# A written order of all five engines, from the first gate tile through the second chunk of a linear-attention and gated-feed-forward kernel

## The chip, the cores and the metric

One core of a Trainium2 chip runs the whole kernel. The metric is the device time of one execution in microseconds; the time of a kernel is the median of several. The core has five engines that each work through their own list of instructions in order: PE (TensorE, matmul; its weight loads are counted apart as PEld), DVE (VectorE), ACT (ScalarE), POOL (GpSimd) and SP (SyncE, which here issues all DMAs). They wait for each other on semaphores.

## The reference

```python
def _attn_ref(q, k, v):                 # (batch 8, heads 8, seq 576, head_dim 64)
    q_s = exp(q - max(q, axis=-1));  q_s = q_s / (sum(q_s, axis=-1) + 1e-09)
    k_s = exp(k - max(k, axis=2));   k_s = k_s / (sum(k_s, axis=2) + 1e-09)
    kv = einsum('bhsd,bhse->bhde', k_s, v)
    return einsum('bhsd,bhde->bhse', q_s, kv)

x = attn_out.transpose(0, 2, 1, 3).reshape(4608, 512)
a = x @ w_a                             # 512 x 1536
b = x @ w_b                             # 512 x 1536
out = (a * b) @ w_out                   # 1536 x 512
```

Everything is float32; the weights arrive as 64-bit floats, and the kernel turns them into float32 itself.

## The kernel before

**Tiling.** The 4608 rows of x are cut into nine chunks of 512. The 1536 inner columns are cut into twelve tiles f of 128 (six pairs i). For precision a float32 operand is split into two parts in a format that PE reads fast ("hi" and "lo", `split`: a copy on ACT, a subtraction on DVE), and a product is three matmuls: hi·hi, hi·lo, lo·hi.

**Start-up and first chunk (chunk 0).** `Startup` is a class of small steps, named by two letters and numbers (`wl20`: the lo part of weight tile 2, first half). They are traced in the order of a hand-written string: keys (`mc`, `ek`, `tr`, `pk`, `kv`), queries (`qs`, `qe`, `pq`, `px`), operands of x (`xh`, `xl`), weights (`wc`, `ws`, `wa`, `wo`, `wh`, `wl`: the conversion of one 128 x 512 block goes ACT, DVE, POOL, DVE, ACT, DVE) and the first three gate tiles (`g`, `ga`, `G`).

Then a loop over f = 2 to 11 does for each f:

- load the raw weights of tile f + 2 (`load_f`; three loads of 512 KB on SP);
- convert weights: `convert_wo(f)` for the output weights, `convert_ab(f + 1, 0)` and `(f + 1, 1)` for the two gate halves;
- of a task n = f - 3 the transposes ("turn"), of task n + 1 the softmax ("soft"); the nine tasks are key pairs 0 to 3 and query pairs 0 to 3 of the second chunk, and one key pair of the third;
- the gate tile f: 24 matmuls of 128 x 512 into two banks (`gate_part`, twelve for a, twelve for b), ACT copies a out (`gate_half`), DVE multiplies by b (`gate_end`);
- the product of task n ("prod"), and the projection of tile f - 1 into four banks (`project_first`, four float32 matmuls).

**From the second chunk on (chunks 1 to 8)** a pair i takes seven half-size products (`product`, twelve matmuls of 128 x 256 each) into banks kx, ky, ka and kp, with sums and products on DVE (u2, u3, cc), a hi/lo split (`g_split`) and a projection of twelve matmuls a tile (`project`). Between them `attend` (a `Spread`) traces a share of the attention of the chunk after. In chunk 1 the operands S1 to S4 are sums of weight blocks that POOL adds (`sums`) and that ACT and DVE split.

**What sets the order.** A scheduler orders the traced instructions by a timeline of its own and by priorities. Three things bound it: `in_order` chains what lies in a stretch of the trace by dependences without a semaphore, so that an engine takes it in the order of the code (ACT, DVE and POOL in the hand-written start-up, SP in its loads, PE from the start to the end of the first chunk); `tc.issue_after(x)` lets what is traced in it go only behind x (weights of tile f + 1 behind the end of gate tile f - 2, the softmax likewise, and in `attend` the attention pieces behind the last DVE operation of the products); and the buffers.

Of the kernel before, what the change touches and what calls it, by code (L numbers as in the profile page):

```python
# [25 lines left out]
P1, P6, P7, P5, P2, P3, P4 = range(7)  # L26


@with_exitstack
def linear_attention_then_gated_ffn(  # L30
# [570 lines left out]
    xfs = {}  # L601
# [91 lines left out]
    class Spread:  # L693
# [5 lines left out]
        def __call__(self, behind=None):  # L699
# [3 lines left out]
            with ExitStack() as pinned:  # L703
                if behind is not None:
# [284 lines left out]
    traced = nc.cur_bb.bb.instructions  # L989
    by_hand = len(traced)  # L990
    for step in (
# [9 lines left out]
        getattr(Startup, name)(*(int(n) for n in step[len(name):]))  # L1001
# [20 lines left out]

    in_order((E.SP,), loads, by_hand)
    in_order((E.Activation, E.DVE, E.Pool), by_hand, len(traced))
    startup = [at["last", 0].ins, at["last", 1].ins]
# [3 lines left out]
    for f in range(2, NF):  # L1029
        if 1 < f - 1 < NF - 3:  # L1030
            tasks[f - 1][0]()
        if f + 2 < NF:
            load_f(f + 2)

        with tc.issue_after(at["end", f - 2].ins):
            convert_wo(f)
            if f + 1 < NF:
                convert_ab(f + 1, 0)
                convert_ab(f + 1, 1)


        n = f - 3
        if n < 0:
            copies = ()
        else:
            copies = tasks[n][2]()
        if n + 1 < NF - 3:
            with tc.issue_after(startup[0]), tc.issue_after(at["end", max(f - 2, 1)].ins):
                tasks[n + 1][1]()
        if f == NF - 1:  # L1050
            with tc.issue_after(at["end", f - 1].ins):
                split_wo(0)
                split_wo(1)
            sy[0] = sums(0)
        if f > 2:
            pts = gate_banks(("k0", "k1"))
            for h in range(2):
                gate_part(f, x0, h, range(NP), pts[h])
                if h == 0:
                    with ExitStack() as pinned:  # L1060
                        for copy in copies or ():
                            pinned.enter_context(tc.issue_after(copy.ins))
                        at["ga", f] = gate_half(f, pts[0])
            at["end", f] = gate_end(at["ga", f], pts[1])
        if 0 <= n < len(tasks):
            tasks[n][3]()
        if f == NF - 2:
            x_operands(xfs[1], early + late, xo)
        project_first(*pending, po)
        pending = (f, at["ga", f])  # L1070
    in_order((E.PE,), by_hand, len(traced))
# [15 lines left out]
    for c in range(1, NCH):  # L1087
# [4 lines left out]
        for i in range(NI):  # L1092
            def operand(op):
                if c > 1:
                    return get_w(i, op)
                if op in (A11, A12, A22):
                    return get_w(i, op)
                w = split_w(sy[i][op])
                put_w(i, op, w)
                return w  # L1100

            if more and i == NI - 1:
                x_operands(xfs[c + 1], early, xo)
# [5 lines left out]
            u3 = sb.tile([P, 2, H], F32, name="u3", bufs=1)  # L1109
            if c > 1 or i > 0:  # L1110
                attend(last)
# [92 lines left out]
```

## Time and profile before

| | |
|---|---|
| median of 3 runs | 964.56 us (964.27 to 965.41) |
| profiled execution, its own time | 966.23 us |
| its span, first to last instruction | 964.4 us |
| mean granted clock of PE | 0.998 |
| busy in the span: PE / PEld / DVE / ACT / POOL | 932.9 / 828.2 / 624.6 / 391.5 / 105.5 us |
| DMA read and written | 241.40 MB, 37.98 MB |

The profile is one execution, taken by the hardware's profiler. A timeline row gives start and duration in microseconds, engine, line of the kernel, operation, what it writes and reads, its size, how many follow each other, and in brackets the idle time of that engine just before, with what ended it. Line numbers are those of the kernel before: L537 is the gate matmul, L572 the projection of the first chunk, L562 the half-size products, L583 the projection of the later chunks, L846 and L299 key transposes, L314 the key product, L468 and L904 query transposes, L481 the query product, L271 a product with ones that spreads a maximum; L946 and L82 are lo splits on DVE, L548 the gate product, L292 and L385 maxima of a softmax, L110 the addition on POOL in a weight conversion, L225 the sums of weight blocks.

### The profile page before, as it was taken

What the parts mean: (1) busy time and instruction counts of PE and PEld (TensorE: products, weight loads), DVE (VectorE), ACT (ScalarE), POOL (GpSimd) and SP (SyncE); (2) the same over time, 40 slices, a digit from 0 to 9 for tenths busy, and PEclk for the clock granted to TensorE, in tenths of its full rate; (3) what the DMA queues carried; (4) which work ended last, traced back from release to release, by engine and by line L of the source; (5) the groups of instructions that cost most, each with busy time, mean ns of one, the idle gap of its engine ahead of it and who ended that gap; (6) DMA issues with size and microseconds to landing.
All of it is one profiled execution on the core that took longest, in us unless ns stands there. A gap on an engine that the chain in (4) does not pass through costs nothing.

```text
span 964.4 us, 17587 instructions
## 1 busy us (share of the span) xinstructions
PE 932.9 (97%) x6479; PEld 828.2 (86%) x6479; DVE 624.6 (65%) x1209; ACT 391.5 (41%) x1085; POOL 105.5 (11%) x88
## 2 busy tenths in 40 slices
PE   5899999899999999999999999999999999999998
PEld 3656656889999999989999999999999999999997
DVE  7987878886686747665566657566666547553433
ACT  7787744452372416322443244223622263221111
POOL 1544342422000000000000000000000000000000
PEclk9999999999999999999999999999999999999999
DMA  9999686989998968897799779877987689667761
GB/s 348 412 381 390 214 274 214 407 276 332 323 357 297 359 238 273 305 368 256 258 330 356 268 244 351 316 280 258 344 304 286 240 289 305 243 236 266 258 211 56
DMA packets 97588, 282.64 MB, mean 293 GB/s; under 512 B 11680, under 2 KB 12256, under 8 KB 97504
## 3 DMA queue, kind: packets, MB, share of 16 engines
q1 hardware_dynamic: 97504, 281.52, 81.6%
q8 instruction: 52, 0.85, 0.3%
q14 instruction: 32, 0.26, 0.1%
HBM read 241.40 MB, written 37.98 MB: 290 GB/s over the span
## 4 chain that ended last, share of the span: by engine, by line
PE 79%; DVE 7%; DMA 5%; issue 4%; POOL 2%; ACT 2%; SPq 1%; DVEq 0%; POOLq 0%
PE po L583 27%; PE kp L562 13%; PE ka L562 13%; PE kx L562 13%; PE ky L562 7%; POOL wr L110 2%; PE px L493 2%; PE pk L314 2%; DMA ws<-dw 1%; DMA raw<-in_w_ab 1%; DVE wy L113 1%; PE pt L537 1%; DMA ws_y<-dy 1%; SPq L448 1%; DMA kt_first<-in_kt 1%
## 5 line engine op out<-in xcount | busy, mean ns | idle before, releaser
L583 PE MATMUL po<-wo_w,gh 128*128 128x512 f32 x768 | 226.3, 395 | 1.0 <-ACT gh L79 1.0
L562 PE MATMUL kx<-xo,ws 128*128 128x256 f32 x1152 | 162.7, 283 | 0.0
L583 PEld LDWEIGHTS po<-wo_w,gh 128*128 128x128 f32 x768 | 138.6, 188 | 27.6 <-ACT gh L79 1.5
L562 PE MATMUL ka<-xo,ws 128*128 128x256 f32 x1152 | 160.9, 282 | 0.4 <-DVE cc L1147 0.4
L562 PE MATMUL kp<-xo,ws 128*128 128x256 f32 x1152 | 157.6, 283 | 1.5 <-DVE u L1120 1.5
L562 PEld LDWEIGHTS ka<-xo,ws 128*128 128x128 f32 x1152 | 149.5, 188 | 4.7 <-DVE cc L1147 0.6
L562 PEld LDWEIGHTS kp<-xo,ws 128*128 128x128 f32 x1152 | 147.7, 188 | 5.2 <-issue 1.6
L562 PEld LDWEIGHTS kx<-xo,ws 128*128 128x128 f32 x1152 | 149.5, 188 | 2.5
L583 PE MATMUL po<-wo_w,gl 128*128 128x512 f32 x384 | 136.4, 396 | 0.0
L79 ACT CAST gh<-cc 128x512 fp32r<-128x512 f32 x96 | 56.6, 620 | 134.5 <-DVE cc L1144 128.2
L1143 DVE TENSOR_TENSOR cc<-kp,u 128x512 f32<-128x512 f32 x48 | 33.1, 689 | 99.1 <-PE kp L562 98.9
L1134 ACT COPY cc<-kx 128x256 f32<-128x256 f32 x48 | 17.8, 371 | 182.9 <-PE kx L562 182.8
L583 PEld LDWEIGHTS po<-wo_w,gl 128*128 128x128 f32 x384 | 71.2, 188 | 16.0 <-DVE gl L82 0.4
L407 ACT ACTIVATE qt<-qt,st 128x64 f32<-128x64 f32 x224 | 75.0, 339 | 22.4 <-DVE st L404 17.2
L1133 DVE TENSOR_TENSOR cc<-kp,u 128x512 f32<-128x512 f32 x48 | 33.1, 689 | 76.1 <-PE kp L562 75.9
L562 PE MATMUL ky<-xo,ws 128*128 128x256 f32 x576 | 77.6, 284 | 3.2 <-DMA ws<-dw 2.2
L562 PEld LDWEIGHTS ky<-xo,ws 128*128 128x128 f32 x576 | 71.9, 188 | 4.5 <-DVE gl L82 2.1
L82 DVE TENSOR_TENSOR gl<-cc,gh 128x512 fp32r<-128x512 f32 x96 | 64.6, 692 | 10.6 <-ACT gh L79 10.6
L537 PE MATMUL pt<-xo,ws 128*128 128x512 f32 x288 | 70.2, 399 | 1.1 <-DVE ws L946 1.1
L244 POOL PARTITION_ALL_REDUCE mx<-m x20 | 18.3, 915 | 446.5 <-DVE m L255 446.5
L537 PEld LDWEIGHTS pt<-xo,ws 128*128 128x128 f32 x288 | 53.5, 189 | 14.0 <-DVE ws L946 1.6
L1119 ACT COPY u<-kx 128x512 f32<-128x512 f32 x48 | 28.0, 584 | 84.6 <-PE kx L562 84.3
(147 smaller groups left out, 1155.6 us busy)
## 6 DMA issues: line engine op xcount, KB each, us to landing
ws<-dw SPq DMA_DIRECT2D x312, 512.0 KB, 5.5
dw<-ws SPq DMA_DIRECT2D x42, 512.0 KB, 7.2
mr<-dq SPq DMA_DIRECT2D x112, 128.0 KB, 4.6
raw<-in_w_ab SPq DMA_DIRECT2D x24, 512.0 KB, 8.0
out<-ot SPq DMA_DIRECT2D x36, 256.0 KB, 4.7
vt<-in_v SPq DMA_DIRECT2D x28, 325.0 KB, 6.9
qt<-in_q SPq DMA_DIRECT2D x32, 256.0 KB, 5.5
kt<-in_k SPq DMA_DIRECT2D x24, 320.0 KB, 5.1
```

Source lines behind the costliest of these rows:

```text
L79: nc.scalar.copy(out=hi, in_=src)
L82: return nc.vector.tensor_tensor(out=lo, in0=src, in1=hi.bitcast(F32), op=ALU.subtract)
L110: nc.gpsimd.tensor_tensor(out=r, in0=u, in1=r, op=ALU.add)
L314: nc.tensor.matmul(pk[h * D:(h + 1) * D], kt[:, j, h], vt[:, j, h], start=(j == 0), stop=(j == J - 1),)
L407: nc.scalar.activation(out=qt[:, j, h], in_=qt[:, j, h], func=AF.Exp, bias=st[:, h, 0, j:j + 1], accum_out=st[:, h, 1, j:j + 1],)
L493: nc.tensor.matmul(px[:, s], w, m[:, s], start=(i == 0), stop=(i == 2))
L537: nc.tensor.matmul(pt, w[:, wp], x[g][:, xp], start=(g == 0 and i == 0), stop=(g == NP - 1 and i == 2),)
L562: ins = nc.tensor.matmul(pt[:, n], w[:, n, wp, c], x[:, xp, c], start=(first and n == 0 and i == 0), stop=(i == 5), skip_group_check=True,)
L583: ins = nc.tensor.matmul(po[t], a[:, ts], wo[f][:, w], start=(f == 0 and i == 0), stop=(f == NF - 1 and i == 2),)
L1119: nc.scalar.copy(out=u2, in_=kx)
L1133: nc.vector.tensor_tensor(out=cc[:, 3], in0=kp, in1=u3, op=ALU.add)
L1143: nc.vector.tensor_tensor(out=cc[:, 1], in0=kp, in1=u2, op=ALU.add)
```

## The change

Every piece that is traced from the start-up on gets a name (`named`): the step's own name in the start-up; `load.f`, `raw.f`, `out.f`, `a.f`, `b.f`, `turn.n`, `soft.n`, `split.m`, `sums.i`, `gate.f`, `prod.n`, `x.1`, `proj.f` in the loop; and in chunks 1 and 2 `w<op>.i`, `pair.i`, `proj.i`, `attend.i` and so on, with i counted on from 0 to 11. `ORDER` holds for each of the five engines a list of these names; `name*3` takes the next three instructions of that piece on that engine, `name:9` the one that stands tenth among those left. `arrange` chains an engine's instructions in the order of its list; what the list leaves out of the rest of the program goes behind its last entry, in the scheduler's order. The `issue_after` pins of the loop are gone, and `attend` is pinned only from chunk 2 on. No instruction is added, removed or changed on any engine, and no buffer.

```diff
+ORDER = {
+    "PE": (
...
+        "gate.10:9 turn.7*4 gate.10:9 gate.10:9 gate.10:9 proj.8 gate.10*12 proj.8 proj.9:1 proj.9:2 "
...
+    "Activation": (
...
+        "turn.5 b.10 soft.7 soft.7:1 turn.6 soft.7 split.9 soft.7:1 b.11 soft.7:2 out.11 soft.7:2 "
...
+    @contextmanager
+    def named(name):
+        before = traced[-1]
+        yield
+        start = next(n for n in reversed(range(len(traced))) if traced[n] is before) + 1
+        for ins in traced[start:]:
+            work.setdefault((ins.engine, name), []).append(ins)
...
-    in_order((E.SP,), loads, by_hand)
-    in_order((E.Activation, E.DVE, E.Pool), by_hand, len(traced))
...
+    def behind_each_other(instructions):
+        for ins, before in zip(instructions[1:], instructions):
+            tc.add_manual_dep(ins, before.name, ..., reason="in order")
+
+    def arrange(engine, names):
+        left = {name: list(found) for (of, name), found in work.items() if of == engine}
+        chain = []
+        for item in names.split():
+            name, _, count = item.partition("*")
+            name, _, place = name.partition(":")
+            for _ in range(int(count or 1)):
+                chain.append(left[name].pop(int(place or 0)))
+        behind_each_other(chain)
+        placed = {ins.name for ins in chain}
+        for ins in traced[by_hand:]:
+            if ins.engine == engine and ins.name not in placed:
+                behind_each_other([chain[-1], ins])
+
+    behind_each_other([ins for ins in traced[loads:by_hand] if ins.engine == E.SP])
...
-        with tc.issue_after(at["end", f - 2].ins):
+        with named(f"out.{f}"):
             convert_wo(f)
...
-            with tc.issue_after(startup[0]), tc.issue_after(at["end", max(f - 2, 1)].ins):
+            with named(f"soft.{n + 1}"):
                 tasks[n + 1][1]()
...
-    in_order((E.PE,), by_hand, len(traced))
...
-                attend(last)
+                with part("attend"):
+                    attend(c > 1 and last)
...
+    for engine, names in ORDER.items():
+        arrange(getattr(E, engine), names)
```

What this does to the lists of the engines is seen at three places. On PE it moves instructions from the first gate tile to a place early in the third chunk, and behind that the list is as it was; SP's list is the same until three weight loads of the second to third chunk change places with attention loads.

DVE at the first gate tiles, before. `ws_432` and `ws_474` are the lo splits of the two halves of weight tile 2, `ga_470` the gate product of tile 0, `yo0` and `yo1` output weights, `wy_427` a weight block in conversion.

```order
L946 TENSOR_TENSOR ws_432<-wy_318,ws_432 128x2x256
L107 TENSOR_SCALAR wo0_raw_105<-yo0_364 128x512
L107 TENSOR_SCALAR wo1_raw_111<-yo1_370 128x512
L113 SCALAR_TENSOR_TENSOR wy_427<-wy_427,wr_428 128x512
L548 TENSOR_TENSOR ga_470<-pt1_347,ga_470 128x512
L107 TENSOR_SCALAR wo2_raw_114<-yo_529 128x512
L113 SCALAR_TENSOR_TENSOR yo0_364<-yo0_364,wr_365 128x512
L946 TENSOR_TENSOR ws_474<-wy_427,ws_474 128x2x256
```

DVE at the same place with the change. `mc_620` is a maximum of key pair 1, `raw_120` and `raw_122` belong to weight tile 3, `ga_482` is the gate product of tile 1.

```order
L1073 TENSOR_TENSOR ws_432<-wy_318,ws_432 128x2x256
L240 SCALAR_TENSOR_TENSOR wy_427<-wy_427,wr_428 128x512
L234 TENSOR_SCALAR wo2_raw_114<-yo_529 128x512
L234 TENSOR_SCALAR wo1_raw_111<-yo1_370 128x512
L240 SCALAR_TENSOR_TENSOR yo0_364<-yo0_364,wr_365 128x512
L675 TENSOR_TENSOR ga_470<-pt1_347,ga_470 128x512
L419 TENSOR_REDUCE mc_620<-kt_126 128x1
L234 TENSOR_SCALAR raw_120<-wy_536 128x512
L675 TENSOR_TENSOR ga_482<-pt1_411,ga_482 128x512
L240 SCALAR_TENSOR_TENSOR yo1_370<-yo1_370,wr_371 128x512
L234 TENSOR_SCALAR raw_122<-wy_548 128x512
L1073 TENSOR_TENSOR ws_474<-wy_427,ws_474 128x2x256
```

Five operations have moved in ahead of `ws_474` and one more in ahead of `ga_470`; three more maxima (of key pair 0 and query pairs 0 and 1) now stand straight ahead of `ws_432`.

PE at gate tile 3, before: the transposes of key pair 0 (`pka`, `pkb`), the tile (banks `pt_623` and `pt_624`), the product of key pair 0 (`pk`), the projection of tile 2 into `po_512` to `po_515`.

```order
L299 MATMUL pka<-ident,kt 128x128 x4
L299 MATMUL pkb<-ident,kt 128x128
L537 MATMUL pt_623<-xo,ws 128x512 x12
L537 MATMUL pt_624<-xo,ws 128x512 x12
L314 MATMUL pk<-vt,kt 64x65 x10
L572 MATMUL po_512<-yo,ga 128x512
L572 MATMUL po_513<-yo,ga 128x512
L572 MATMUL po_514<-yo,ga 128x512
L572 MATMUL po_515<-yo,ga 128x512
```

With the change; `pka` already stands further up, among the matmuls of tiles 1 and 2.

```order
L664 MATMUL pt_623<-xo,ws 128x512 x3
L426 MATMUL pkb<-ident,kt 128x128
L699 MATMUL po_513<-yo_370,ga 128x512
L664 MATMUL pt_623<-xo,ws 128x512 x3
L664 MATMUL pt_624<-xo,ws 128x512 x9
L699 MATMUL po_512<-yo,ga 128x512
L664 MATMUL pt_623<-xo,ws 128x512 x3
L664 MATMUL pt_624<-xo,ws 128x512 x3
L699 MATMUL po_515<-yo,ga 128x512
L699 MATMUL po_513<-yo,ga 128x512
L699 MATMUL po_514<-yo,ga 128x512
L441 MATMUL pk<-vt,kt 64x65 x10
```

The tile is cut into groups, projections of two tiles have moved in among them, and `pk` has moved behind the projection of tile 2.

PE at the seam from the first to the second chunk, before: the end of gate tile 11 (`pt_1451`, `pt_1452`), the first product `kx` of the second chunk, the spread maximum `pmx`, the projection of tile 10, the second product `ky`. The product of the last query pair stands further up, ahead of tile 11.

```order
L537 MATMUL pt_1451<-xo,ws 128x512 x12
L537 MATMUL pt_1452<-xo,ws 128x512 x12
L562 MATMUL kx<-xo,ws 128x256 x12
L271 MATMUL pmx<-m_1431,ones 128x128
L572 MATMUL po_512<-wo_w,ga 128x512
L572 MATMUL po_513<-wo_w,ga 128x512
L572 MATMUL po_514<-wo_w,ga 128x512
L572 MATMUL po_515<-wo_w,ga 128x512
L562 MATMUL ky<-xo,ws 128x256 x12
```

With the change; the two `px` rows are the product of the last query pair.

```order
L608 MATMUL px<-qw,wholes 128x64
L608 MATMUL px<-qw,wholes 128x448
L699 MATMUL po_514<-wo_w,ga 128x512
L699 MATMUL po_512<-wo_w,ga 128x512
L689 MATMUL kx<-xo,ws 128x256 x12
L664 MATMUL pt_1452<-xo,ws 128x512 x6
L699 MATMUL po_513<-wo_w,ga 128x512
L398 MATMUL pmx<-m_1431,ones 128x128
L699 MATMUL po_514<-wo_w,ga 128x512
L699 MATMUL po_515<-wo_w,ga 128x512
L689 MATMUL ky<-xo,ws 128x256 x12
```

`px` has moved down to just ahead of `kx`, and six gate matmuls and a projection product have moved in between `kx` and `pmx`.

More of the change, by code (lines that the diff above doesn't have):

```diff
@@ L1055, in linear_attention_then_gated_ffn @@
-        if f > 2:
[L1056 to L1062, printed above, removed]
+            for m in range(2):
+                with named(f"split.{m}"):
+                    split_wo(m)
+            with named("sums.0"):
+                sy[0] = sums(0)
@@ L1109, in linear_attention_then_gated_ffn, with multiply @@
             u3 = sb.tile([P, 2, H], F32, name="u3", bufs=1)
+            def multiply(pt, op, xop, first):
+                w = operand(op)
+                with part("pair"):
+                    return product(pt, w, x[xop], first)
             if c > 1 or i > 0:
-                attend(last)
+                with part("attend"):
+                    attend(c > 1 and last)
             if c == 1:
                 if i + 1 < NI:
-                    sy[i + 1] = sums(i + 1)
-                    split_wo(2 * i + 2)
-                    split_wo(2 * i + 3)
@@ L1117, in linear_attention_then_gated_ffn @@
-            product(kx, operand(A11), x[B11], True)
-            product(ky, operand(S2), x[T2], True)
-            nc.scalar.copy(out=u2, in_=kx)
-            nc.vector.tensor_tensor(out=u2, in0=ky, in1=u2, op=ALU.add)
-            product(ka, operand(S3), x[T3], True)
-            last = nc.vector.tensor_tensor(out=u3, in0=ka, in1=u2, op=ALU.add)
+                    with part("sums"):
+                        sy[i + 1] = sums(i + 1)
+                    for f in (2 * i + 2, 2 * i + 3):
+                        with named(f"split.{f}"):
+                            split_wo(f)
@@ L1123, in linear_attention_then_gated_ffn @@
+            multiply(kx, A11, B11, True)
+            multiply(ky, S2, T2, True)
+            with part("pair"):
+                nc.scalar.copy(out=u2, in_=kx)
+                nc.vector.tensor_tensor(out=u2, in0=ky, in1=u2, op=ALU.add)
+            multiply(ka, S3, T3, True)
+            with part("pair"):
+                last = nc.vector.tensor_tensor(out=u3, in0=ka, in1=u2, op=ALU.add)
             if more and i == NI - 1:
-                x_operands(xfs[c + 1], late, xo)
+                with part("late"):
+                    x_operands(xfs[c + 1], late, xo)
@@ L1125, in linear_attention_then_gated_ffn @@
             end = c == NCH - 1 and i == NI - 1
             if not end:
-                run_pending()
-            attend(last)
+                with part("proj"):
+                    run_pending()
+            with part("attend"):
+                attend(c > 1 and last)
             kp = ps.tile([P, 2, H], F32, name="kp", tag="k1")
-            product(kp, operand(S1), x[T1], True)
-            product(kx, operand(A12), x[B21], False)
-            nc.vector.tensor_tensor(out=cc[:, 3], in0=kp, in1=u3, op=ALU.add)
@@ L1137, in linear_attention_then_gated_ffn @@
             if not end:
[L1138 removed]
+                with part("proj"):
+                    run_pending()
             if po is None:
                 po = [ps.tile([P, DM], F32, name=f"po{t}") for t in range(TT)]
[L1141 to L1145 removed]
@@ L1146, in linear_attention_then_gated_ffn @@
-            last_product = product(ka, operand(A22), x[T4], False)
-            nc.vector.tensor_tensor(out=cc[:, 2], in0=ka, in1=u2, op=ALU.add)
-            last = nc.vector.tensor_tensor(out=cc[:, 2, 0], in0=cc[:, 2, 0], in1=cc[:, 2, 1], op=ALU.mult)
-            g2 = g_split(2 * i + 1, cc[:, 2:4, 0])
+            with part("attend"):
+                attend(c > 1 and last)
+            multiply(kp, S4, B22, False)
+            with part("pair"):
+                nc.vector.tensor_tensor(out=cc[:, 1], in0=kp, in1=u2, op=ALU.add)
+                nc.vector.tensor_tensor(out=cc[:, 1, 0], in0=cc[:, 1, 0], in1=cc[:, 1, 1], op=ALU.mult)
+                g1 = g_split(2 * i, cc[:, 0:2, 0])
```

114 lines of the change are left out of this document (65 added, 49 removed), and 113 rows, old and new, of the table ORDER.

## The prediction

> **What bounds the kernel now.** I read first the page's busy times, then the span cut into windows, then who waited for whom on PE, then PE's own timeline around each wait, and last DVE's and ACT's timelines just ahead of those waits.
>
> ```profile
> PE 932.9 (97%) x6479; PEld 828.2 (86%) x6479; DVE 624.6 (65%) x1209; ACT 391.5 (41%) x1085; POOL 105.5 (11%) x88
> ```
>
> PE (TensorE) carries the kernel. No instruction is added or removed on it, so only PE's idle time, or time at a lower clock, can be gained. The windows (span and length; then busy us and count of PE, PEld, DVE, ACT, POOL; clock, DMA share, GB/s) say where that is.
>
> ```profile
> 25.00:50.00 25.00, 23.24 (x110) 16.91 (x111) 24.64 (x38) 18.60 (x35) 12.77 (x9) 1.00 1.03 413
> 25.00:200.00 175.00, 161.30 (x828) 115.56 (x829) 143.78 (x250) 114.68 (x295) 73.73 (x52) 0.99 0.87 326
> 200.00:300.00 100.00, 100.00 (x768) 92.94 (x767) 78.48 (x158) 43.83 (x125) 11.91 (x10) 1.00 0.94 326
> ```
>
> From 200 us on PE is busy 100.00 of 100: reordering there can lose but not win. Up to 24 us the changed order is the old one. From 25 to 200 us PE stands still for 175.00 - 161.30 = 13.70 us. Whom it waits for there (us, times, longest):
>
> ```profile
> PE pq L468 <- DVE qt L394: 2.2, 1, 2.2
> PE pmx L271 <- DVE m L265: 2.0, 1, 2.0
> PE pk L314 <- ACT kt L300: 1.9, 1, 1.9
> PE pka L299 <- ACT kt L293: 1.5, 1, 1.5
> PE kp L562 <- DVE u L1120: 1.5, 1, 1.5
> PE pt L537 <- DVE ws L946: 1.1, 1, 1.1
> PE po L583 <- ACT gh L79: 1.0, 1, 1.0
> PE ky L562 <- DVE cc L1143: 0.7, 1, 0.7
> PE ka L562 <- DVE cc L1147: 0.4, 1, 0.4
> ```
>
> Nine single waits (two shorter ones follow), each on one small transpose or product behind a softmax or a gate, while independent gate matmuls stand behind it in PE's fixed order. That is latency, not a full engine: DVE is busy 143.78 of 175 us (82%). Only in 25 to 50 us is DVE full (24.64 of 25).
>
> **Part 1, key pair 0 and the clock (gate tile 3).**
>
> ```profile
> 54.92 5.82 PE L537 MATMUL pt<-xo,ws 128*128 128x512 f32 x24
> 62.67 0.80 PE L314 MATMUL pk<-vt,kt 128*64 128x65 f32 x20 [1.94 <-ACT kt L300]
> 63.41 5.40 PE L572 MATMUL po<-yo,ga 128*128 128x512 f32 x8
> 69.62 0.30 PE L299 MATMUL pkb<-ident,kt 128*128 128x128 f32 x1 [0.38 <-DVE wholes L325]
> 76.16 3.70 PE L572 MATMUL po<-yo,ga 128*128 128x512 f32 x8
> 60.00:63.40 3.40, 1.46 (x24) 0.93 (x22) 2.43 (x3) 3.40 (x14) 2.35 (x2) 1.00 0.99 352
> 63.50:66.80 3.30, 3.30 (x4) 1.41 (x5) 3.23 (x7) 3.29 (x8) 1.27 (x1) 0.50 1.02 405
> ```
>
> Before, the key product of 10 (x20 in the trace) follows gate tile 3 and waits 1.94 us for a copy that stands behind seven exponentials and a split on ACT. Now one projection product comes before the last gate matmuls of the tile and three behind them, ahead of the key product: 3 x 3.70/4 = 2.8 us of ready work, more than the wait. The second wait, 0.38, has gate tile 5 around it now. Gain 2.32. The row after the wait shows the price of the pause: the granted clock is 0.50 for one stretch, and the projection takes 5.40 instead of 3.70. With no pause, 1.70 more. I take it whole: the stretch just ahead, with PE busy 1.46 of 3.40, is the emptiest after the start. Ends: 0 and 4.02.
>
> [...]
>
> **Part 2, key pair 2 and query pair 3.**
>
> ```profile
> 91.75 0.66 PE L299 MATMUL pka<-ident,kt 128*128 128x128 f32 x4 [1.47 <-ACT kt L293]
> 136.02 0.63 PE L468 MATMUL pq<-ident,qt 128*128 128x128 f32 x4 [2.22 <-DVE qt L394]
> 132.04 1.52 ACT qt L388 x9
> ```
>
> Both transposes stood at the head of a gate tile. Now two groups of three matmuls of the same tile stand ahead of the first and three ahead of the second, 0.73 us a group (5.82/24 x 3): 1.5 and 2.2 us of cover, just the waits. The softmax moves too: before, ACT copied gate tile 9's half and then ran the eight exponentials (the last row, from the chain of waits, is their end); now all eight stand ahead of that copy, spread among weight splits. Gain 1.47 + 2.22 = 3.69; ends 0 and 3.69. If the tile's own weights are late the cover is gone, and the loss is priced in Part 6.
>
> **Part 3, the front (tiles 0 to 2).**
>
> ```profile
> 25.62 0.63 PE L904 MATMUL pq<-ident,qts 128*128 128x128 f32 x4 [1.68 <-issue]
> 30.42 1.99 PE L481 MATMUL px<-qw,wholes 128*128 128x512 f32 x4
> 30.52 2.96 DVE L946 TENSOR_TENSOR ws<-wy,ws 128x512 fp32r<-128x512 f32 x3
> 39.90 0.68 DVE L548 TENSOR_TENSOR ga<-pt,ga 128x512 f32<-128x512 f32 x1
> 43.76 3.99 PE L537 MATMUL pt<-xo,ws 128*128 128x512 f32 x16 [1.11 <-DVE ws L946]
> 46.61 1.53 DVE L292 TENSOR_REDUCE mc<-kt 128x1 f32<-128x640 f32 x2
> 57.25 0.67 DVE L385 TENSOR_REDUCE qst<-qt 128x8 f32<-128x512 f32 x1
> 41.94 1.76 DVE L946 TENSOR_TENSOR ws<-wy,ws 128x512 fp32r<-128x512 f32 x1
> ```
>
> Three gate matmuls now fill part of the 1.68 us gap and the key scaling runs earlier, so the last start-up products (second row) end about 1.2 sooner, at 31.2; the wait of 1.11 goes as well, since the second half of tile 2 now comes last. Against that stand 0.77 + 2 x 0.67 = 2.1 us of maxima on a full DVE, ahead of a weight split, and one more join (0.68) ahead of the gate product of tile 0: it starts at 39.90 + 2.1 + 0.7 = 42.7 and ends at 43.4. PE asks for it after the 36 remaining matmuls of tiles 0 and 1 (8.7 us from 31.2) and three of tile 2 (0.7), plus 1.0 of waits on splits, at 41.6: a wait of 1.8. Everything on PE stands behind that wait. Three groups of three now follow straight on their split (0.98 each in the third row); I charge half, 1.5. Net 2.3 - 3.3 = **-1.0**. Ends: +2.3, and -4.3 if the maxima delay every split. The split of tile 2's second half ended at 43.7; the three maxima, another key maximum, two shifts, one join and another gate product, 5.1 us, make it 48.8, but its matmuls are asked for at about 50: nothing.
>
> What queues behind it: on SP (SyncE), whose order stays as it was until after 300 us, that split's store stands ahead of half of tile 6's loads, which then go some 5 us later; tile 6 begins only behind the transpose at 91.75.
>
> **Part 4, the seam to the second chunk.**
>
> ```profile
> 142.07 1.14 PE L481 MATMUL px<-qw,wholes 128*128 128x64 f32 x4
> 155.78 0.46 PE L271 MATMUL pmx<-m,ones 128*128 128x128 f32 x2 [2.04 <-DVE m L265]
> 144.57 0.68 DVE L511 TENSOR_TENSOR xt<-xf,xt 128x512 f32<-128x512 f32 x1
> 148.25 1.78 DVE L521 TENSOR_TENSOR xt<-xf,xt 128x512 f32<-128x512 f32 x1
> 146.27 6.62 POOL L225 TENSOR_TENSOR ws_y<-ws_y 128x512 f32<-128x512 f32 x4 [2.77 <-DMA ws_y<-dy]
> ```
>
> The wait of 2.04 goes: six gate matmuls and one projection product now follow the first product of the pair. But the last query product (first row) moves from ahead of gate tile 11 to behind most of it, so product ky comes only two projection products, one pair product, six gate matmuls, and three projection products later: 5 x 0.9 + 1.5 (12 of half the columns) + 1.5 = 7.5 us. Its operand needs one ACT copy (0.6) and, in DVE's list, nine operations up to its own split: 0.6 + 9 x 0.7 = 6.9 us at 0.68 each. They cost 1.78 when they run beside POOL's sums (last rows); two of them so make it 9.1, a wait of 1.6. I take the middle, about 1.0: net **+1.0**, ends +2.0 and -2.5. Behind ky queue ka, kp and the whole pair, and DVE's sum u waits with them.
>
> [...]
>
> **Part 5, the second chunk.** The waits on kp, po, ky, ka and kt add up to 1.5 + 1.0 + 0.7 + 0.4 + 0.2 = 3.8 us. Projection pieces now stand between the products of a pair. The elementwise rows they wait for stay on a busy DVE, so I take two thirds: **+2.5**; ends 0 and 3.8.
>
> **Part 6, waits that nobody has yet seen.** From 70 to 145 us the list cuts each tile into groups, and all compute engines must now keep in step: gate copies and products stand in DVE's and ACT's lists where the list expects PE to be, and weight conversions queue behind them. The front shows 3.3 us of such waits in 20 us with DVE full; with DVE at 82% I charge **-1.5**; ends 0 and -8. One later wait may move, since two weight loads on SP now go ahead of three attention loads near 318 us:
>
> ```profile
> 416.87 1.66 PE L562 MATMUL ky<-xo,ws 128*128 128x256 f32 x12 [1.96 <-DMA ws<-dw]
> ```
>
> It stands behind other loads, so I leave it; ends +2 and -2.
>
> Sum: 2.32 + 1.70 + 3.69 - 1.0 + 1.0 + 2.5 - 1.5 = 8.7 us. The profiled execution took 966.23 us (964.4 span and 1.8 around it), 1.7 above the median, 964.56. So 957.5 by the profile's scale, **955.9** by the median's.
>
> **Rivals.**
>
> (a) All of it: no new waits. 13.70 + 1.70 = 15.4 gained, 949.2. For it: each wait is single and has ready work beside it. Against: Part 3's count. Chance 0.17.
>
> (b) The supply of weights takes the place of PE's order: PE runs ahead and then waits. The chain of waits goes through loads of raw weights.
>
> ```profile
> 86.68 6.32 DMA raw<-in_w_ab
> 135.68 0.69 DVE L82 TENSOR_TENSOR ws<-wy,ws 128x512 fp32r<-128x512 f32 x1
> 146.50 5.82 PE L537 MATMUL pt<-xo,ws 128*128 128x512 f32 x24
> ```
>
> Then only Part 5 stays: 962.0. Against: tile 11's weights are split at 136.4, 10 us ahead of its first matmul, more than the gain. Chance 0.12.
>
> (c) The clock drop is not due to that pause and stays: 957.6. Chance 0.12.
>
> (d) Slower: the fixed lists miss each other all the way as in the front, 3.3 us in each 20 us from 45 to 152 us: 17.7 lost against 12.2 (Parts 1, 2, 5, the whole seam wait and 1.7 of clock counted) less 1.0: 971.1. It decides from about 11 us of new waits. Against: DVE has 31 us free between 25 and 200 us. Chance 0.08.
>
> (e) Nothing: latencies move but PE's stalls reappear at the next transpose: 964.5. Chance 0.05.
>
> **How the numbers follow.** The likeliest, 955.9, has 0.46, its own range 951 to 960. A change under 0.2% (1.9 us) can hardly be told from none here. Of (b), a quarter falls within that. Faster 0.46 + 0.17 + 0.12 + 0.09 = 0.84; same 0.08; slower 0.08. The range runs from (a), 949.0, to just past (b), 962.5, leaving out (d) and (e).
>
> **What would show it.** Right: the key product behind tile 3 with no wait; clock 1.00 from 60 to 70 us; no wait at the transposes of key pair 2 and query pair 3; PE idle 25 to 200 us near 7 us; the seam reached some 6 us sooner. Wrong: waits of several us on weight splits in tiles 4 to 10, a wait of more than 3 us at ky, another stretch at clock 0.50, or idle after 200 us.

## The result, and the profile after

The changed kernel takes 957.51 us (median of six runs, 956.13 to 960.93) against 964.64 for the kernel before: ratio 0.9931, 95% interval 0.9913 to 0.9950. A second set of runs (e5) gave 958.18 us and 0.9923 (0.9907 to 0.9940). By the ratios that is 6.6 to 7.4 us faster; 955.9 had been forecast. The profiled execution, at 956.13 us, is the fastest of its set, so it shows more gain (10.1 us against the profile before, 966.23) than the medians do.

Busy times of the page after:

```profile
PE 931.9 (98%) x6479; PEld 827.2 (87%) x6479; DVE 613.4 (64%) x1209; ACT 390.6 (41%) x1085; POOL 105.3 (11%) x88
```

PE does the same work; DVE is 11 us less busy with the same 1209 instructions. A stretch at half clock (0.50 from 18.15 to 21.56 us) in the start-up, whose order is the old one, stays out of what follows; the profile before has none there (1.00 from 0 to 25 us). Windows of the profile before (the first three) and after (the last five), columns as in the prediction: span and length, then busy us and count of PE, PEld, DVE, ACT, POOL, then clock, DMA share, GB/s.

```profile
25.00:150.00 125.00, 117.23 (x524) 78.79 (x525) 103.66 (x168) 87.30 (x200) 56.20 (x40) 0.99 0.86 324
150.00:200.00 50.00, 44.07 (x306) 36.77 (x305) 40.13 (x84) 27.38 (x95) 17.53 (x13) 1.00 0.88 329
300.00:950.00 650.00, 647.50 (x4745) 602.22 (x4745) 380.42 (x758) 210.79 (x607) 14.89 (x16) 1.00 0.80 282
...
25.00:50.00 25.00, 24.38 (x114) 16.98 (x113) 22.84 (x42) 21.89 (x46) 12.98 (x10) 1.00 1.03 410
25.00:150.00 125.00, 123.81 (x567) 83.74 (x566) 103.96 (x178) 92.61 (x218) 59.34 (x42) 1.00 0.95 353
150.00:200.00 50.00, 48.69 (x360) 43.15 (x359) 40.03 (x96) 24.72 (x84) 15.98 (x11) 1.00 0.86 304
200.00:300.00 100.00, 96.50 (x736) 88.15 (x735) 70.86 (x146) 40.46 (x119) 10.47 (x9) 0.98 0.95 326
300.00:950.00 650.00, 649.31 (x4727) 602.92 (x4726) 380.09 (x754) 212.66 (x610) 14.90 (x16) 1.00 0.79 278
```

PE's idle time: 7.77 us become 1.19 from 25 to 150 us (6.6 gained, and 1.7 of half clock), 5.93 become 1.31 from 150 to 200 (4.6 gained), none becomes 3.50 from 200 to 300 (3.5 lost), 2.50 become 0.69 from 300 on (1.8 gained). From 25 to 200 us together 13.70 become 2.49, where the forecast had about 7. And a stretch at half clock is back, in another place. PE's timeline after, with the copy on ACT that the key product needs as second row; then the windows around the pause in the last row:

```profile
40.68 1.90 PE L699 MATMUL po<-yo,ga 128*128 128x512 f32 x4
48.74 0.57 ACT L427 COPY kt<-pka 128x512 f32<-128x512 f32 x1
59.42 2.74 PE L699 MATMUL po<-yo,ga 128*128 128x512 f32 x6
62.09 0.80 PE L441 MATMUL pk<-vt,kt 128*64 128x65 f32 x20
148.17 1.56 PE L689 MATMUL ky<-xo,ws 128*128 128x256 f32 x11 [0.15 <-DVE xo L209]
217.68 1.47 PE L689 MATMUL ka<-xo,ws 128*128 128x256 f32 x10 [1.02 <-DVE cc L1317]
252.63 0.33 PE L620 MATMUL px<-qh,kvh 128*128 128x128 f32 x1 [2.09 <-ACT qh L206]
```

```profile
250.26:253.67 3.41, 1.32 (x12) 1.12 (x10) 1.75 (x3) 1.25 (x2) 0.00 (x0) 1.00 1.02 406
253.67:257.09 3.42, 3.42 (x14) 3.13 (x13) 3.42 (x8) 1.65 (x3) 0.00 (x0) 0.50 0.94 357
```

The projection of tile 0 (first row) and the key product (fourth row) wait for nothing, ky for 0.15 us. The new pause stands at the start of the third chunk: px, the last attention product of that chunk, waits 2.09 us for its softmax, and the clock is 0.50 for the 3.42 us behind it. Pause and half clock together are 3.8 us; of all that is lost behind 200 us this is the largest piece.

### The profile page after: what moved, and what is told of

It reads as the page before. It is cut to its first block, busy times and chain, and to the rows that moved or that the text cites. A ratio compares the mean times of both kernels' runs of the same rounds, so it can differ in the third digit from the quotient of the medians.

```text
span 954.4 us, 17546 instructions
## 1 busy us (share of the span) xinstructions
PE 931.9 (98%) x6479; PEld 827.2 (87%) x6479; DVE 613.4 (64%) x1209; ACT 390.6 (41%) x1085; POOL 105.3 (11%) x88
## 4 chain that ended last, share of the span: by engine, by line
PE 88%; DMA 4%; DVE 4%; ACT 1%; SPq 1%; issue 1%; POOL 0%; POOLq 0%; DVEq 0%; ACTq 0%
PE po L710 27%; PE kx L689 14%; PE kp L689 14%; PE ka L689 14%; PE ky L689 7%; PE pt L664 5%; PE po L699 3%; PE px L620 2%; PE pk L441 2%; DMA mr<-dq 2%; DMA kt_first<-in_kt 1%; DMA ws_y<-dy 1%; DVE ws L209 1%; DMA ws<-dw 1%; DVE wo_w L209 0%
## 5 line engine op out<-in xcount | busy, mean ns | idle before, releaser
L710 PE MATMUL po<-wo_w,gh 128*128 128x512 f32 x768 | 228.1, 396 | 0.0
L689 PE MATMUL kx<-xo,ws 128*128 128x256 f32 x1152 | 164.2, 284 | 0.5 <-ACT u L1281 0.3
L689 PE MATMUL ka<-xo,ws 128*128 128x256 f32 x1152 | 160.8, 282 | 2.1 <-DVE cc L1317 1.0
L710 PEld LDWEIGHTS po<-wo_w,gh 128*128 128x128 f32 x768 | 138.0, 189 | 25.7 <-ACT gh L206 0.3
L689 PE MATMUL kp<-xo,ws 128*128 128x256 f32 x1152 | 157.2, 282 | 0.0
L689 PEld LDWEIGHTS ka<-xo,ws 128*128 128x128 f32 x1152 | 149.7, 188 | 7.1 <-DVE cc L1317 1.2
L689 PEld LDWEIGHTS kx<-xo,ws 128*128 128x128 f32 x1152 | 149.7, 189 | 5.4 <-ACT qt L534 1.0
L689 PEld LDWEIGHTS kp<-xo,ws 128*128 128x128 f32 x1152 | 148.2, 188 | 4.3 <-DVE cc L1299 0.3
L710 PE MATMUL po<-wo_w,gl 128*128 128x512 f32 x384 | 137.7, 396 | 0.0
L710 PEld LDWEIGHTS po<-wo_w,gl 128*128 128x128 f32 x384 | 71.2, 188 | 15.8 <-DVE gl L209 0.4
L664 PE MATMUL pt<-xo,ws 128*128 128x512 f32 x288 | 83.7, 432 | 0.5 <-DVE xo L1048 0.5
L689 PE MATMUL ky<-xo,ws 128*128 128x256 f32 x576 | 76.9, 282 | 0.8 <-DMA ws<-dw 0.7
L689 PEld LDWEIGHTS ky<-xo,ws 128*128 128x128 f32 x576 | 72.1, 188 | 2.2 <-DVE xf L806 0.9
L209 DVE TENSOR_TENSOR gl<-cc,gh 128x512 fp32r<-128x512 f32 x96 | 63.9, 685 | 13.3 <-ACT gh L206 10.7
L664 PEld LDWEIGHTS pt<-xo,ws 128*128 128x128 f32 x288 | 53.1, 189 | 22.1 <-issue 9.5
```

Of the source, the lines that this page charges most:

```text
L209: return nc.vector.tensor_tensor(out=lo, in0=src, in1=hi.bitcast(F32), op=ALU.subtract)
L664: nc.tensor.matmul(pt, w[:, wp], x[g][:, xp], start=(g == 0 and i == 0), stop=(g == NP - 1 and i == 2),)
L689: ins = nc.tensor.matmul(pt[:, n], w[:, n, wp, c], x[:, xp, c], start=(first and n == 0 and i == 0), stop=(i == 5), skip_group_check=True,)
L710: ins = nc.tensor.matmul(po[t], a[:, ts], wo[f][:, w], start=(f == 0 and i == 0), stop=(f == NF - 1 and i == 2),)
```

## The experiments

All lists below are those of the change, edited. Ratios are to the kernel before, with 95% intervals. Line numbers are those of the changed kernel: L664 is the gate matmul, L689 the half-size product, L699 and L710 the projections, L441 the key product, L426 its transposes and L427 the copy of them, L620 px, L209 and L1073 lo splits, L240 joins of a weight conversion, L512 and L419 maxima. In e2 the lines of the later chunks stand 11 further down (L1328 is L1317 of the change).

### e9: is Part 1 the key product and its pause?

```diff
 PE:         "... gate.3:3 proj.2 gate.3*6
-             proj.2:2 proj.2*2 prod.0*10"
+             prod.0*10 proj.2:2 proj.2*2"
 Activation: "... out.4 soft.4
-             turn.0
              a.3 soft.4 ... soft.2:1 a.6 soft.2 b.4
+             turn.0"
```

> The change with the key pair 0 part undone: on PE the key product stands directly behind gate tile 3 again, ahead of three projection products, and on ACT the copy of the transposes stands behind the exponentials and the weight split again, as before the change. From the profile of the change: PE reaches the product at 59.4 us, the copy ends at 62.9 us there, a pause of about 3.4 us. Theory C (the clock drop behind such a pause comes from the pause: the profiles so far show half clock for 3.41 us behind every stretch of the clock's own 3.41 us grid in which PE was idle 1.94 us or more, and none behind one with 1.68 us or less): a drop if 1.9 us or more of the pause fall into one stretch of the grid; 3.4 + up to 1.7 us more than the change, of which later waits take some back: 960 to 963 us. Rival (the drop before had another cause, and the copy is not what the product waits for): no pause above 1 us, 957.5 to 958.5.

Measured: 964.29 us, 0.9979 (0.9960 to 0.9998), 0.5 to 0.6% above the change: undoing this one part costs about 5 of the 7 us. PE's timeline at the product, and three windows of 3.41 us, the last of them the stretch at half clock:

```profile
62.60 0.80 PE L441 MATMUL pk<-vt,kt 128*64 128x65 f32 x20 [3.33 <-ACT kt L427]
```

```profile
57.09:60.51 3.42, 2.18 (x8) 1.13 (x6) 3.34 (x7) 1.89 (x5) 0.86 (x2) 1.00 1.02 413
60.51:63.92 3.41, 1.32 (x22) 1.02 (x23) 2.01 (x3) 3.41 (x11) 3.24 (x3) 1.00 1.04 420
63.92:67.33 3.41, 3.41 (x7) 1.33 (x5) 3.39 (x9) 0.72 (x3) 0.00 (x0) 0.50 1.03 414
```

The pause is back, 3.33 us, and with it the half clock: 1.24 us of idle fall into the first window and the clock stays at 1.00, 2.09 into the second and the next is at 0.50. Pause and clock cost 3.33 + 1.7 = 5.0 us, more than the 1.94 + 1.70 of the kernel before, since PE comes to the product sooner here. The time lies a little above the forecast 960 to 963; Theory C holds, the rival falls. The edit undoes PE's part and ACT's part at once, so it does not say what each is worth alone.

### e1, e2, e6: which stretch of the list pays

```diff
 def arrange(engine, names):
     ...
+    first = {ins.name for ins in traced[by_hand:seam]}       # e1; e2 keeps the others
+    chain = [ins for ins in chain if ins.name in first]
     behind_each_other(chain)
```

In e1 `seam` is the end of the first chunk, and in e6 the start of the third pair of the second; from there `attend` is pinned as before, and only PE's later work goes behind the list. In e2 the first chunk has its old pins, and on PE its old order. What no list holds, the scheduler orders anew: in e2 DVE, ACT and SP depart from the kernel before between 51 and 56 us, and in e1 ACT and DVE take operations of the rest in between from 46 and 48 us on.

> The written order holds only up to the last instruction of the first chunk; from there the scheduler orders all engines and the attention pieces are pinned behind DVE's products again, as before the change. Theory A (the gain is made in the first chunk: PE stands still 8.8 us less between 25 and 150 us; what the list of the second chunk wins between 150 and 200 us, 5.1 us, is given back between 200 and 300 us, 6.5 us): 954 to 957 us, no worse than the whole change at 957.5. Rival B (the second chunk's list is worth its 5 us and the loss behind 200 us has another cause): about 962.

> The reverse: first chunk as before (pins and order of the code), written order only for what is traced from the second chunk on. Theory S (the loss between 200 and 300 us comes from PE running further ahead than the loads in SP's queue): PE is only some 4 us ahead here, so the 3.8 to 5.1 us won between 150 and 200 us are kept, 959.5 to 961 us, and no wait of 2 us before the query product at the start of the third chunk. Rival (the list of the second and third chunk itself holds the pauses): a pause of about 2 us and a stretch at half clock there all the same, 963 to 966.

> The written order holds through the first chunk and the first two pairs of the second; from the third pair on the scheduler orders, with the attention pinned behind DVE's products as before. Theory L (the list itself holds the pauses between 185 and 260 us, since it fixes places that the scheduler left open: e1, which has no list there, lost 0.73 us between 200 and 300 us where the change lost 3.5 and a clock drop; and the list is what saves the 2.07 and 2.72 us that e1 loses at 158 and 172 us): the better half of each, 952.5 to 954.5 us. Rival D (the loads are the limit, so what is won at 158 and 172 us is lost again at the next weights): 957 to 960.

Measured: e1 960.56 us, 0.9942 (0.9925 to 0.9960); e2 976.57, 1.0115 (1.0097 to 1.0132); e6 966.65, 1.0008 (0.9992 to 1.0024). All three missed their numbers. (The 8.8, 5.1 and 6.5 us that e1 started from are not in the windows, which give 6.6, 4.6 and 3.5 of idle time, and 8.3, 4.6 and 5.2 with the half clock.) The windows of e1:

```profile
150.00:200.00 50.00, 44.80 (x333) 39.68 (x332) 45.36 (x87) 26.29 (x94) 18.19 (x12) 1.00 0.79 294
200.00:300.00 100.00, 99.27 (x775) 91.55 (x774) 74.49 (x155) 42.55 (x121) 9.37 (x8) 1.00 0.93 321
```

Without a list behind the first chunk PE idles 5.2 us from 150 to 200 us and 0.7 from there to 300; with it 1.3 and 3.5, and a half clock. So the second chunk's list wins 3.9 and loses 2.8 + 1.7 in these profiles; by the ratios (0.9942 against 0.9931 and 0.9923) it is worth 1 to 2 us, which the intervals don't separate from nothing. The first chunk's list is worth 0.6% alone.

In e2 PE comes to the third chunk 20 us later than in the change, and yet it waits at the same places:

```profile
203.87 1.66 PE L689 MATMUL ka<-xo,ws 128*128 128x256 f32 x12 [1.29 <-DMA ws<-dw]
236.83 1.46 PE L689 MATMUL ka<-xo,ws 128*128 128x256 f32 x10 [0.55 <-DVE cc L1328]
272.99 0.33 PE L620 MATMUL px<-qh,kvh 128*128 128x128 f32 x1 [2.12 <-ACT qh L206]
```

```profile
268.60:272.02 3.42, 2.27 (x20) 2.06 (x18) 0.69 (x1) 0.36 (x1) 0.00 (x0) 1.00 0.98 303
272.02:275.43 3.41, 2.31 (x16) 2.10 (x16) 2.46 (x5) 1.09 (x3) 0.00 (x0) 1.00 1.02 393
275.43:278.84 3.41, 2.94 (x13) 2.41 (x14) 3.33 (x7) 2.30 (x5) 0.00 (x0) 1.00 1.02 374
```

That ends Theory S as I had put it: PE does not outrun the loads; the pause belongs to the order itself. A detail on the clock: the same pause, 2.12 us, here falls across two windows of 3.41 us (1.15 and 1.10 idle), and the clock stays at 1.00. Why e2 as a whole is slower is seen in part: PE idles 10.1 us from 25 to 150 us, 3.6 to 200 and 7.6 to 300 (before: 7.8, 5.9 and 0), and one more stretch is at half clock (0.97 from 150 to 200 us, where before has 1.00), together 9.3 us, where the two spans differ by 10.1.

e6 has no pause at px, but PE loses 14 us where the list ends:

```profile
185.09 1.35 PE L441 MATMUL pk<-vt,kt 128*64 128x65 f32 x20 [4.63 <-ACT kt L406]
192.00 0.48 PE L388 MATMUL pm<-ident,m 128*128 128x128 f32 x1 [3.09 <-DVE m L382]
...
150.00:200.00 50.00, 35.88 (x267) 30.64 (x266) 36.06 (x87) 22.30 (x79) 17.04 (x12) 0.83 0.81 295
```

The waits are those of attention steps of the third chunk, one behind the other. The cut goes through the middle of that attention; neither theory had this, and which step of the cut causes it stays open. PE is late behind it, so e6 says nothing on the pauses after 200 us.

### e3, e7: PE's list, or the others?

```diff
-for engine, names in ORDER.items():
+for engine, names in ORDER.items():        # e3: PE alone, with the old pins for the rest
+    if engine == "PE":                     # e7: all, but PE's first chunk in the order of the code
         arrange(getattr(E, engine), names)
```

The block is an outline: e7 has all the lists, and in PE's the first chunk is put in the order of the code. In e3 the old pins don't bring back the old lists: DVE departs from the kernel before at 40 us, ACT at 46, SP at 53, so e3 shows PE's list with what the scheduler makes of the rest.

> PE's written list alone; ACT, DVE, POOL and SP ordered as before the change, with its pins. Theory A (PE's list covers each latency with ready work, the other lists only keep step): more than half of the gain stays, 957 to 961 us. Rival (the engines must move together, since the list expects exponentials, copies and splits at their new places): new waits of several us on PE in 45 to 150 us, 966 us or more.

> The reverse of e3: the written lists of ACT, DVE, POOL and SP, and PE's from the second chunk on; in the first chunk PE takes its work in the order of the code, as before. Theory A (PE's list is what covers the waits): the transposes and products wait again, 963 us or more. Rival B (the earlier exponentials and copies on ACT and DVE make the operands ready in time, whatever PE's order): 960 us or less, with no wait at the key product behind gate tile 3. e3 lost 8 us against the change in this stretch without those lists, so if e7 is slow as well, neither half works alone.

Measured: e3 969.75 us, 1.0042 (1.0025 to 1.0059); e7 997.82, 1.0330 (1.0309 to 1.0350). The first two rows are e3's, the others e7's:

```profile
46.56 0.66 PE L426 MATMUL pka<-ident,kt 128*128 128x128 f32 x4 [2.08 <-ACT kt L420]
79.82 0.96 PE L664 MATMUL pt<-xo,ws 128*128 128x512 f32 x3 [3.05 <-ACT ga L671]
...
85.29 0.59 ACT L671 COPY ga<-pt 128x512 f32<-128x512 f32 x1 [7.40 <-PE pt L664]
93.20 1.35 PE L441 MATMUL pk<-vt,kt 128*64 128x65 f32 x20 [4.93 <-ACT wy L230]
```

In e3 PE asks for transposes whose exponentials ACT takes only at 45.7 us. In e7 it is the other way round: ACT stands still 7.40 us for a gate tile that PE has not reached, all that its list has behind that copy is late, and then PE waits 4.93 us for ACT at the key product. Theory A of e3 and Rival B of e7 fall: neither PE's list nor the others carry the gain alone. PE's list without the others takes 0.4% more than the kernel before and the others without PE's first chunk 3.3% more, where the whole set takes 0.7 to 0.8% less.

### e8: why did the maxima not delay the front?

```diff
 DVE: "...
-      soft.0 soft.2 soft.4 wl20
+      wl20 soft.0 soft.2 soft.4
       wo21 ..."
```

> The change with one edit on DVE: the lo split of weight tile 2's first half stands ahead of the three softmax maxima at 35 to 37 us instead of behind them, beside two additions of POOL. Theory P (operations with two inputs from SBUF take longer beside POOL's additions and those with one input don't, so the maxima fill time that a split would have spent waiting): the split takes 1.3 to 2.2 us instead of 0.76, and the gate product of tile 0 starts less than 0.8 us earlier or not at all. Rival (the maxima cost what they take): the split takes 0.7, and the rest as before.

Measured (one profile, 957.5 us), the first three rows on DVE, then the gate product of tile 0 on DVE and what PE makes of it:

```profile
35.05 0.91 DVE L1073 TENSOR_TENSOR ws<-wy,ws 128x512 fp32r<-128x512 f32 x1 [0.43 <-ACT ws L1068]
35.88 0.81 DVE L419 TENSOR_REDUCE mc<-kt 128x1 f32<-128x640 f32 x1
36.61 1.26 DVE L512 TENSOR_REDUCE qst<-qt 128x8 f32<-128x512 f32 x2
...
40.11 0.68 DVE L675 TENSOR_TENSOR ga<-pt,ga 128x512 f32<-128x512 f32 x1
40.84 1.98 PE L699 MATMUL po<-yo,ga 128*128 128x512 f32 x4 [0.66 <-DVE ga L675]
```

With the split ahead, it waits 0.43 us for ACT and takes 0.91 instead of 0.76; the gate product is no earlier (39.85 in the change), though the operations ahead run 0.7 us earlier in this profile, and PE waits 0.66 for it. So the maxima fill 0.6 of the 2.1 us that they take with time that the split would have spent on ACT and beside POOL. They stand ahead of the gate product in both orders, so its start doesn't give their price. Of Theory P the second half holds and the size, 1.3 to 2.2, does not, and that operations with one input keep their time beside POOL is not shown as a rule (a shift at 43.68 takes 1.51 there); why they did not delay the front is answered below, by DVE's durations.

### e4, e5, e10: the pause at px

```diff
 SP: "... attend.3*4 attend.4
+     attend.4*4
      w5.5 w6.5 w0.6 w1.6
-     attend.4*4
      w2.6 w3.6 ..."
```

> The whole change with one edit: the four loads of softmax rows (mr) of the last query pair of the third chunk go four places earlier in SP's queue, ahead of one weight store and three 512 KB weight loads. Every other list is unchanged. Theory S (the 2.09 us pause at 252.6 us and the half clock behind it, 1.70 us, come from those loads standing behind 1.5 MB of weights): both go, 957.5 - 3.8 = 953.7 us. Rival (the pause is a fixed latency, or moves on to the next operand): 956.5 to 958.5.

> The changed kernel itself, once more, beside the runs that follow and with a second profile. The runs of the change spread over 4.8 us (956.13 to 960.93), those of e4 over 0.8, and the profile of e4 shows waits on weight loads of 1.14, 0.66, 1.58 and 1.38 us between 184 and 225 us, ahead of its edit, where the first profile of the change shows two of 0.92 and 1.02 on DVE. Theory D (between 180 and 260 us PE stands at the edge of what the loads deliver, and the time depends on how each run's transfers fall): median 956.5 to 958.5 again with a spread above 3 us, and in this profile other waits there than in the first. Rival (the list is met the same way each time, and the spread is noise elsewhere): the same two waits and the same pause of 2.1 us at the start of the third chunk, with the half clock behind it.

> e4 once more, with a second profile, beside e9 and e11. If the earlier softmax loads are worth what e4 showed: ratio to before 0.988 to 0.991, again no pause of 2 us and no half clock at the start of the third chunk. If e4 was luck of the runs: 0.992 to 0.994, as the change itself.

Measured: e4 955.73 us, 0.9896 (0.9879 to 0.9914); e10, the same kernel, 955.43, 0.9884 (0.9856 to 0.9913); e5, the change, 958.18, 0.9923. SP's queue in the change (two rows), then in e4 (two rows) with px there; then e5's two largest waits, and px in e8 and e9, which keep the change's order of SP:

```profile
236.08 4.58 SPq L335 DMA_DIRECT2D ws<-dw  x3
240.76 2.38 SPq L575 DMA_DIRECT2D mr<-dq  x4
...
235.52 2.38 SPq L575 DMA_DIRECT2D mr<-dq  x4
238.62 3.99 SPq L575 DMA_DIRECT2D mr<-dq  x4
253.18 0.22 PE L620 MATMUL px<-qh,kvh 128*128 128x128 f32 x1
...
179.62 0.59 PE L689 MATMUL ky<-xo,ws 128*128 128x256 f32 x3 [2.08 <-DVE cc L1312]
255.94 0.33 PE L620 MATMUL px<-qh,kvh 128*128 128x128 f32 x1 [2.33 <-ACT qh L206]
...
254.56 0.33 PE L620 MATMUL px<-qh,kvh 128*128 128x128 f32 x1 [1.29 <-ACT qh L206]
259.48 0.33 PE L620 MATMUL px<-qh,kvh 128*128 128x128 f32 x1 [1.02 <-ACT qh L206]
```

From the issue of the loads to PE's turn at px the change has 9.8 us (240.76 to 252.63 less the 2.09 waited), e5 9.9 and e2, 20 us later in all, 9.8 again (261.08 to 270.87): each time too little by 2.1 to 2.3; e4 has 14.6 (238.62 to 253.18), and px waits for nothing, with no half clock behind it (1.00 from 250 to 300 us). That PE comes to px later in e4 and e5 than in the first profile of the change, through waits before 225 us, doesn't explain it, since e5 pauses all the same. e10 is as e4, with 0.85 us at the px before. The mean of the two ratios is 0.37% below that of the change, 3.6 us, of 3.8 expected; by the medians as they stand (955.73 and 955.43 against 957.51 and 958.18) it is 2.3 us, and the intervals overlap a little. So the place in SP's queue sets this pause. e5 decides between D and its rival in part: px pauses again, 2.33 us with the half clock behind it (0.50 from 257.36 to 260.77 us), and the runs spread over 1.8 us, not above 3; but the waits of 0.4 to 2.1 us between 175 and 225 us differ from profile to profile. The size of the pause does too. In e8 and e9 px waits 1.29 and 1.02 us, with no half clock behind it (its next matmuls of 384 columns on `ql` and `kvl` take 0.34 us each, 0.52 in the change), and PE's turn comes 10.8 and 10.4 us after the issue. In all of these the operand is there 11.4 to 12.2 us after the issue, and what varies is when PE asks; so a price of about 4 us holds for the two profiles of the change (after, e5) and not for every execution.

### e11, e12: more of the same

e11 puts three weight loads ahead of the loads for POOL's sums, e12 puts ready projections ahead of four products; both build on e4.

```diff
 SP (e11): "... w2.3 w3.3
-           sums.4*2 w4.3 w6.3 w5.3 sums.4 w0.4
+           w4.3 w6.3 w5.3 w0.4 sums.4*3 ..."
 PE (e12), one of four:
-          "pair.2*24 proj.1*2 proj.1:1 pair.2*12 ..."
+          "pair.2*12 proj.1*2 proj.1:1 pair.2*24 ..."
```

> e4 with one more edit in SP's queue at the fourth pair of the second chunk: three weight loads (512 KB each) and one weight store go ahead of three loads of 256 KB for POOL's sums. In e4's profile two products kx wait there 0.66 and 1.58 us for weight loads that stand behind these, and ACT and DVE behind them make later products wait 0.44 and 1.38. Theory Q (these waits are the loads' place in the queue; 0.75 MB at the 350 to 410 GB/s that the windows show are 1.8 to 2.1 us): the two waits go, 953 to 954.5 us. Rival (the transfers are limited here whatever the order, and the sums come late in turn): 955 to 957, with the wait moved to products ky or ka, whose operands are the sums.

> e4 with four edits in PE's list and nothing else: at the four products of the third and fifth pair of the second chunk that waited 1.1 to 1.6 us in e4's two profiles (ky at 179, ka at 186, the two kx at 213 and 225 us), two to four projection matmuls that stood right behind the product now stand ahead of it (0.7 us of ready work each, and 1.2 us with a key product at the third). Theory A (a wait is gone as far as ready work stands ahead of it): 0.7 + 0.7 + 1.2 + 0.7 = up to 3.3 us of cover, of which the operands behind these products, which then come later, take some back: ratio to before 0.985 to 0.988 (e4: 0.9896 and 0.9884). Rival (the operands stand on a chain over DVE, ACT and SP that ends when it ends, so the waits reappear at the next product): 0.988 to 0.990, no better than e4.

Measured: e11 957.56 us, 0.9897 (0.9867 to 0.9926); e12 955.56, 0.9897 (0.9881 to 0.9914). No better than e4. The three rows of e11, on PE, DVE and POOL, and one of e12:

```profile
220.72 2.50 PE L689 MATMUL ka<-xo,ws 128*128 128x256 f32 x10 [4.43 <-DVE cc L1317]
218.64 1.09 DVE L209 TENSOR_TENSOR ws<-ws_y,ws 128x512 fp32r<-128x512 f32 x1 [4.34 <-ACT ws L206]
212.53 6.66 POOL L352 TENSOR_TENSOR ws_y<-ws_y 128x512 f32<-128x512 f32 x5 [21.02 <-DMA ws_y<-dy]
...
218.33 1.45 PE L689 MATMUL ka<-xo,ws 128*128 128x256 f32 x10 [1.69 <-DVE cc L1317]
```

In e11 the waits on weights are gone, but the sums come late: POOL, then ACT's and DVE's split, then the product that stands behind that split on DVE, and ka waits 4.43 us. In e12 two of the four waits are gone, two are down to 0.52 and 0.31, and ka waits 1.69. Both rivals hold: these operands end a chain through four engines, and the order moves the wait along it. e4, the simplest, stays the best version.

## Why the prediction came out as it did

The forecast, 955.9, lies 1.6 to 2.3 us below the medians, inside its range. The mechanism is right, latencies covered by work that is ready, but the closeness is in part luck: up to 200 us the profile gained 12.9 us (11.2 of idle time, 1.7 of clock) where 8.7 had been forecast, and behind it lost 3.4 where nothing had been forecast. Two errors of about 4 us cancel.

- **Part 1 (+4.02).** Right in size, and the largest piece: the waits of 1.94 and 0.38 us and the half clock are gone, and to undo it costs 5.0 us by e9's profile, 4.6 to 5.4 by the ratios. The cause was only half right. I let three projections cover the copy; in fact the copy ends at 49.3 us, and DVE's copy of the last transpose at 54.5, 7.6 us ahead of the product, since ACT has its copy ahead of most of the exponentials and PE has the transposes earlier. The projections alone would have left about 0.6 us, an estimate from e9's rows (3.33 less their 2.74). The half clock goes with the pause in these profiles (0.50 behind it before and in e9, 1.00 from 50 to 75 us after), as assumed; rival (c) falls.
- **Part 2 (+3.69).** No wait at either transpose: all of PE's idle time from 25 to 150 us is 1.19 us. Both terms are whole.
- **Part 3 (-1.0).** Wrong sign: from 25 to 50 us PE's idle time fell from 1.76 to 0.62 us, +1.1. The failed step is the count of 2.1 us of maxima and of splits at 0.98 and 1.76 us on a full DVE. DVE's groups in that stretch, before (two rows) and after (three):

```profile
L946 DVE TENSOR_TENSOR ws<-wy,ws 128x512 fp32r<-128x512 f32 x5 | 6.5, 1329 | 0.2 <-ACT ws L941 0.2
L113 DVE SCALAR_TENSOR_TENSOR wy<-wy,wr 128x512 int32<-128x512 int32 x6 | 6.1, 1044 | 0.0
...
L240 DVE SCALAR_TENSOR_TENSOR wy<-wy,wr 128x512 int32<-128x512 int32 x6 | 4.0, 678 | 0.0
L1073 DVE TENSOR_TENSOR ws<-wy,ws 128x512 fp32r<-128x512 f32 x5 | 3.5, 701 | 0.4 <-ACT ws L1068 0.4
L512 DVE TENSOR_REDUCE qst<-qt 128x8 f32<-128x512 f32 x2 | 1.3, 675 | 0.0
```

  Five splits and six joins took 12.6 us and now take 7.5 (three other joins rose from 2.0 to 3.4). Three maxima now stand beside POOL's additions from 34.8 to 37.4 us and keep their time (0.81 us, and 1.27 for two), and the next split takes 0.76 at their end; before, a split at 35.84 stood beside such an addition and took 1.76. (Not every operation with one input from SBUF keeps its time: the shift at 43.43 takes 1.52, where others take 0.42.) I had carried the slow durations over to an order that no longer puts these operations there. Why these operations take longer there is not shown; e8's split takes 0.91 beside two such additions, so a place beside POOL need not cost it. That these durations, and not only the filled time, spared the front its wait is read from the two traces; no run isolates it.
- **Part 4 (+1.0).** The wait of 2.04 is gone, and ky waits 0.15 us, not 1.0: its operand is there 7.8 us after px, where I had 6.9 to 9.1, and PE asks after 7.7, where I had 7.5. Worth about +1.9.
- **Part 5 (+2.5).** About right up to 200 us: idle time from 150 to 200 us fell by 4.6, of which the seam's wait of Part 4 is 2.0. The list's own price behind 200 us is not in it.
- **Part 6 (-1.5).** Right in kind, wrong in place and size. From 70 to 145 us the lists keep step; the new waits stand between 200 and 300 us, 3.5 us and a half clock of 1.7. I had written that reordering there could only lose and then charged nothing, because I looked at the pieces that move and not at SP's queue, which does not move: the loads for px kept their place behind 1.5 MB of weights. Against it, the wait at 417 us went, +1.8 from 300 us on. Whether the weight loads that change places did that is not shown: in e3 and e1 the scheduler puts two of them later than before, not earlier, and the wait is there in e3 (1.65 us at 420.5) and not in e1.
- **Rivals.** (a) falls by the pauses behind 200 us, (e) by the time. (b) and (d) are seen only in part: the change waits for weight loads 0 and 1.9 us between 150 and 300 us (after, e5), and the lists miss each other when only some of them hold (e3, e7).

## What to carry to other kernels

Here an order written for one engine was worth nothing without the orders of those that feed it (e3, 1.0042); price the set, and look first at the queue that was left as it was, since here the wait came out again at an operand whose loads still stood in their old place (px, 2.09 us). Read an operation's duration together with what runs beside it: if the change moves it, the duration may not come along (a split took 1.76 us beside POOL's addition before, 0.76 after). And before filling a pause, ask when the operand is ready: here an earlier copy on ACT (its end at 49.3 us) had it ready before the three matmuls that were meant to cover it (59.42).

## What the runs showed of the hardware

What follows is read from windows of this case's profiles; no run was made for the clock alone.

In the profile after, two stretches of 3.41 us have the clock at 0.50; they begin at 18.15 and 253.67 us, 69 times 3.413 apart. In windows of 3.41 us, of which one ends where a stretch at half clock begins, PE is idle just ahead of it for 1.94 us (before, 60.04 to 63.46), 2.09 (after, from 250.26), 2.09 (e9, from 60.51) and 1.98 (e5, from 253.95). Windows with 1.00 behind them have up to 1.87 and 1.84 us of idle time behind the start-up (before, from 152.20 and 415.03), and in the start-up 2.08 (before, from 5.43) and 2.17 (after, from 7.92). So "every stretch" in e9's expectation does not hold for the start-up, and these windows give no limit.

A pause of 2.09 us is followed by 3.42 us at 0.50, by that clock 1.7 us of work (after); one of 2.12 us that falls across two windows (1.15 and 1.10 idle) is followed by 1.00 (e2). Whether the place of a pause in a fixed step of 3.41 us decides this is not shown: after, e9 and e2 agree with it, and no run isolates it.
